# Attention and expert layers on one core: where a pair's last keys, its sums' product and its preparation stand

## The chip, the cores and the metric

The kernel runs on one core of one Trainium2 chip. The metric is the device time of one execution in microseconds (us), the median of several runs. The engines of the core are PE (TensorE, matmuls; PEld its weight loads), DVE (VectorE), ACT (ScalarE), POOL (GpSimd) and SP (SyncE, which issues all DMAs here).

## What is computed

Eight batches of attention with twelve heads, 448 tokens and head size 64, with a sigmoid in place of the softmax, and then two expert layers over all 3584 tokens (768 to 2048 to 768), with an ELU between them:

```python
scores = scale * np.matmul(q, k.transpose(0, 1, 3, 2)) - np.log(S)
attn = 1.0 / (1.0 + np.exp(-scores))
attn_out = np.matmul(attn, v)                      # (8, 12, 448, 64)
x = attn_out.transpose(0, 2, 1, 3).reshape(B * S, H * D)
h = x @ w_in
g = np.where(h > 0.0, h, np.exp(np.minimum(h, 0.0)) - 1.0)
return g @ w_out
```

## The kernel before

**Numbers.** Almost every float32 operand is scaled by a power of two and split into a high and a low float16 part, the high part by ACT and the low one by DVE (`split`, lines 135 to 137). A product is then three matmuls: high by high, low by high, high by low. Batch 0's attention alone is done in float32.

**Pairs.** A batch's twelve heads are done as six pairs of heads; the batches 1 to 7 run in the loop at the end, pair by pair (`hp` 0 to 5, called pair 0 to pair 5). The 448 keys are three tiles of 128 and a remainder of 64, the last keys. `scores(t)` (L390) multiplies key tile t by all queries on PE into a PSUM tile `psc`, of which there are two; `soften(t)` is ACT's sigmoid into `sg` (L398, four buffers); `parts(t)` splits that into `at` (ACT L434, then DVE L435). `last_keys(two)` (L477, tile `pscr`, one of the two `psc` buffers) does the remainder of two neighbouring pairs in one step, so it needs the transposed `qk` of both; its sigmoid goes into `sgr`, and `parts(NC)` splits one pair's half of it into `ar` (ACT L423, DVE L425). `values(t)` (L457) multiplies `at` and `ar` by the values into `pav`, and `finish` splits the result into `xh` on ACT and DVE (L136, L137).

**Preparation of a pair** happens two pairs ahead. DVE takes the greatest magnitudes (`mx`, L140, L318); a matmul with ones sums them over the partitions (the sums' product, tile `pr`, L128); DVE turns it into powers of two (L130, L102, L103, L328) and POOL into the scales `sc` (L334, L329, L332, L302). `scales()` is all this from the product on. `third()` then splits q and k into `nat` and v into `vn` on ACT and DVE, and issues on SP the DMA that transposes `nat` into `qk` (L362). `prepare_next()` issues on SP the loads of the pair two further on and, on DVE, the magnitudes of the next.

**Filler.** Between a pair's steps PE works on the second expert layer of the batch before: `fill(n)` issues n steps of three matmuls each (L577, `po`). An odd batch has 96 such steps (three tiles of tokens by two halves of the columns by 16), an even one 128, since the remaining 64 tokens of two batches make a tile of their own (`po_r`). A pair gets an equal share of what is left, two more in pair 0; `gap` of them stand before the late scores (11 in pair 0, else 5), the rest before the values, and `tail` of them (4, pair 5 only) behind the values.

**First expert layer.** After pair 5, `hidden` rescales the batch's `xh` on DVE (L496, L498) and `moe1` does 16 tiles f of 18 matmuls each (L547, `ph`), with ACT's exp (L559), DVE's two steps of the ELU (L561, L562), and the split into `g` one tile behind. `beside(f)` is called after tile f and holds the one preparation that is done there. Its PSUM tiles come from three buffers that `pr` and `po` share; f 3 and f 8 use others.

**Order.** Inside `tc.manual_schedule` PE, ACT, DVE and SP issue in the order in which the code is written; only POOL's order is a scheduler's. So a line that is moved moves its instructions on every queue. In batch 1, the generator `steps` still splits the second layer's weights (`step(3)` in pairs 0 and 1, the rest in pair 2), on ACT and DVE.

In a batch's even pairs the order is `scores(0)`, the last keys of two pairs, their sigmoids, `parts(0)`; in odd pairs `scores(0)`, `scores(1)` and their softening. Then come two steps of filler, `scales()`, the rest of `gap`, and the late key tiles. `works` says in which pairs a preparation is done: pairs 1 to 5, and pair 0 of batch 1.

Of the kernel before, what the change touches and what calls it, by code (L numbers as in the profile page):

```python
# [34 lines left out]
def attention_ffn(  # L35
# [13 lines left out]
    NP = H // 2  # L49
    NC = S // P  # L50
# [8 lines left out]
    EXACT = 1  # L59
# [313 lines left out]
    class Pair:  # L373
# [35 lines left out]
        def soften(self, g):  # L409
            nb = 2 if g < NC else 1  # L410
            psc = self.psc.pop(g)
            sg = sb.tile([P, 2, S], F32, tag="sg", name=f"sg{g}{self.u}", bufs=SB)
            self.sigmoid(sg[:, :nb], psc[:, :nb, :S])
            self.sg[g] = [sg]
# [53 lines left out]
    def last_keys(two):  # L468

        psc = ps.tile([P, 2, 512], F32, tag="psc", name=f"pscr{two[0].u}", bufs=2)  # L470
        o = slice(S, S + R)
        for n in range(3):
            for i, p in enumerate(two):
                hi, lo = p.qk
                kk, qq = [(hi, hi), (lo, hi), (hi, lo)][n]
                for j in range(2):
                    nc.tensor.matmul(  # L477
                        psc[rows[j ^ i], i, :S], kk[rows[j], o], qq[rows[j], :S],
                        start=(n == 0), stop=(n == 2),
                    )  # L480
        sg = sb.tile([P, 2, S], F32, tag="sg", name=f"sgr{two[0].u}", bufs=SB)
        for i, p in enumerate(two):
            p.sg[NC] = [sg, i]

        def soften():
            for i, p in enumerate(two):
                p.sigmoid(sg[:, i], psc[:, i, :S])

        return soften
# [37 lines left out]
    def moe1(b, g, xh, m, first, beside=None):  # L527
# [8 lines left out]
        for f in range(NF):  # L536
# [28 lines left out]
            if beside:  # L565
                beside(f)
# [27 lines left out]
    def out_scale(b, xs, xp, i=slice(0, NH)):  # L594
        if b % 2 == 0 and i.start == 0:
            oscs[0] = sb.tile([P, 3, NH], F32, tag="osc", name=f"osc{b}", bufs=2)
        j = b % 2
        o = oscs[0][:, j, i]
        nc.gpsimd.tensor_scalar(
            o, wop[:, i], wm[:, 0:1], 2.0 ** (XBITS - XTOP + 2 - GTOP - WTOP),  # L600
            op0=ALU.mult, op1=ALU.mult,
        )
        nc.gpsimd.tensor_scalar(o, o, xs[:, 0, NP - 1 :], xp, op0=ALU.mult, op1=ALU.mult)
        nc.gpsimd.tensor_copy(oscs[0][rows[j], 2, i], o[rows[j]])

    def moe2(b, g, wo):
        j = b % 2
        osc = oscs[0]

        def tokens(b, c):  # L610
            if c < NC:
                return out[b * S : b * S + SM].rearrange("(p c) m -> c p m", c=NC)[c]
            return out[b * S + SM : (b + 1) * S]

        def tile_of(c, i):
            if c < NC:
                return moe2_tile(
                    wo, [(slice(0, P), tokens(b, c))],
                    lambda gj, f: g[:, gj, f, c * P : (c + 1) * P],
                    osc[:, j, i : i + 1], i, f"{b}_{c}_{i}",  # L620
                )
            return moe2_tile(
                wo, [(rows[a], tokens(b - 1 + a, NC)) for a in range(2)],
                lambda gj, f: g[:, gj, f, SM:],
                osc[:, 2, i : i + 1], i, f"{b}_r_{i}",
            )

        for i in range(NH):
            for c in range(NC + j):
                yield from tile_of(c, i)  # L630
# [3 lines left out]
    def step(n):  # L634
        for _ in range(n):
            next(steps, None)
# [7 lines left out]
    def prepare_pair(n):  # L644

        if n >= len(pairs):
            return lambda: lambda: None
        b, hp = pairs[n]
        if hp == 0:
            xs_of[b] = sb.tile([P, 3, NP], F32, tag="xs", name=f"xs{b}", bufs=2)  # L650
        scales = prepare(b, hp, *loaded.pop(n), xs_of[b])

        def second():
            transposed = scales()

            def third():
                ready[n] = transposed()

            return third

        return second
# [12 lines left out]
    def pair_of(n):  # L674
        b, hp = pairs[n]
        if hp == 0:
            xh_of[b] = sb.tile([P, NK, 2, S], F16, tag="xh", name=f"xh{b}")
        return Pair(b, hp, *ready.pop(n), xh_of[b], xs_of[b])

    def hidden(b, beside=None):  # L680

        xh, xs = xh_of.pop(b), xs_of.pop(b)
        whole = rescale(b, xh, xs)
        next(whole)
        yield
        xp, xr, rest = next(whole)
        m = sb.tile([P, 2, NF], F32, tag="msc", name=f"msc{b}")

        def first():
            rest()  # L690
            moe_scales(m, xs, xr)

        moe1(b, g, xh, m, first, beside)
        yield b, xs, xp
# [13 lines left out]
    for n in range(EXACT * NP):  # L708
# [3 lines left out]
        p = pair_of(n)  # L712
# [14 lines left out]
    scales = prepare_pair(EXACT * NP + 2)  # L727
# [8 lines left out]
    def prepare_next():  # L736
        nonlocal prepared, scales
        load_pair(prepared + 2)
        prepared += 1
        scales = prepare_pair(prepared)  # L740

    def beside(f):
        nonlocal third
        if f == 3:
            third = scales()
        if f == 5:
            third()
            prepare_next()

    third = None  # L750
    E = mybir.EngineType
    with tc.manual_schedule(engines={E.PE, E.Activation, E.DVE, E.SP}):
        for b in range(EXACT, B):
            out_scale(*of_moe2, slice(0, 1 if b == EXACT else NH))
            tiles = moe2(b - 1, g, wo)
            left = NF * NH * (NC + (b - 1) % 2)

            def fill(n):
                nonlocal left
                left -= n  # L760
                for _ in range(n):
                    next(tiles, None)

            for hp in range(NP):
                share = left // (NP - hp) + (2 if hp == 0 else 0)
                tail = 4 if hp == NP - 1 else 0
                works = hp > 0 or b == EXACT
                if hp == 0:
                    two = pair_of(b * NP), pair_of(b * NP + 1)
                elif hp % 2 == 0:  # L770
                    two = pair_of(b * NP + hp), pair_of(b * NP + hp + 1)
                p = two[hp % 2]
                p.scores(0)
                if hp % 2 == 0:
                    soften = last_keys(two)
                    p.soften(0)
                    soften()
                    p.parts(0)
                    early_ones, late_ones = (0,), (1, 2)
                else:  # L780
                    p.scores(1)
                    p.soften(0)
                    p.soften(1)
                    p.parts(0)
                    p.parts(1)
                    early_ones, late_ones = (0, 1), (2,)

                gap = 11 if hp == 0 else 5
                fill(2)
                if works:  # L790
                    third = scales()
                fill(gap - 2)
                for t in late_ones:
                    p.scores(t)
                for t in late_ones:
                    p.soften(t)
                    p.parts(t)
                if hp % 2 == 0:
                    p.parts(NC)
                if works:  # L800
                    third()
                    prepare_next()
                if b == EXACT and hp < NC:

                    step(3 if hp < NC - 1 else NF)
                if hp == NP - 1:
                    h = hidden(b, beside if b + 1 < B else None)
                    next(h)
                fill(share - gap - tail)
                if hp % 2 == 0:  # L810
                    two[1].parts(NC)
                for t in range(NC + 1):
                    p.values(t)
                p.finish()
                fill(tail)
                if b == EXACT and hp == NC - 1:
                    out_scale(*of_moe2, slice(1, NH))
            of_moe2 = next(h)
        out_scale(*of_moe2)
        for _ in moe2(B - 1, g, wo):  # L820
            pass
# [30 lines left out]
```

## Time and profile before

| | us |
|---|---|
| runs | 1246.44, 1250.15, 1252.17 (median 1250.15) |
| the profiled execution | 1246.27 |
| its span, first to last instruction | 1244.5 |
| PE busy | 1162.9 (93%) |
| DVE busy | 828.8 (67%) |
| ACT busy | 722.4 (58%) |
| mean granted TensorE clock | 0.983 of full speed |

The span begins with some 174 us of start, batch 0 and the preparation of the weights. From there on a batch's six pairs and its first expert layer follow each other: pairs of batch 1 from 174, its layer from 275, pairs of batch 2 from 331, and so on to the layer of batch 7, which ends at 1177.6; the second layer of batch 7 ends the span. A row of the timeline gives start, duration, engine, line, operation, output and inputs, how many instructions, and in square brackets the idle time of the engine before it with what ended it. Durations of matmuls overlap, so that a group's length is what counts, not the mean of one. The rows that matter are shown with the prediction.

### The profile page before, as it was taken

How to read it: one execution, taken by the hardware profiler on the slowest of the kernel's cores; microseconds unless marked ns; L12 is line 12 of the kernel's file. 1: busy time of each engine (PE TensorE's matmuls, PEld its weight loads, DVE VectorE, ACT ScalarE, POOL GpSimd, SP SyncE). 2: the span in 40 equal slices, each digit the busy share in tenths (PEclk: the TensorE clock that was granted, in tenths of full speed). 3: DMA queues.
4: the chain of work that ended last, by engine and by line, in shares of the span. 5: the costliest groups of instructions: out<-in, count | busy, mean ns of one | idle time of the engine just before them, and what ended most of it. 6: DMA issues, size and time to landing. Idle time of an engine off the chain costs nothing.

```text
span 1244.5 us, 19369 instructions
## 1 busy us (share of the span) xinstructions
PE 1162.9 (93%) x7342; PEld 599.5 (48%) x7342; DVE 828.8 (67%) x1742; ACT 722.4 (58%) x1099; POOL 95.2 (8%) x275
## 2 busy tenths in 40 slices
PE   6879776899999999989999999999999999999998
PEld 2324333445555555445555554444555555445565
DVE  4897878876467765777567765777567865765500
ACT  4965777765566446764566546774466545863400
POOL 1021002010011100110011100110001000000000
PEclk9989996999999999999999999999999999999999
DMA  8945432442024410442024410343024420310000
GB/s 225 283 122 156 162 127 47 106 103 52 1 58 90 96 39 7 89 109 57 8 58 90 96 38 8 83 96 64 21 51 96 96 38 1 73 28 7 1 26 26
DMA packets 219550, 91.32 MB, mean 73 GB/s; under 512 B 183616, under 2 KB 215360, under 8 KB 219456
## 3 DMA queue, kind: packets, MB, share of 16 engines
q1 hardware_dynamic: 219456, 90.09, 30.1%
q8 instruction: 57, 0.93, 0.3%
q14 instruction: 37, 0.30, 0.1%
HBM read 59.77 MB, written 11.01 MB: 57 GB/s over the span
## 4 chain that ended last, share of the span: by engine, by line
PE 69%; DVE 12%; ACT 7%; DMA 6%; issue 2%; SPq 2%; POOL 1%; DVEq 0%; ACTq 0%
PE ph L547 31%; PE po L577 22%; PE po_r L577 5%; PE pav L457 5%; PE psc L390 5%; DMA qk<-nat 3%; ACT sg L398 2%; DVE at L435 2%; DMA stage<-in_moe_w_in_dram 2%; DVE mx L140 2%; DVE nat L137 1%; DVE ar L425 1%; PE pscr L477 1%; ACT at L434 1%; DMA wo<-in_moe_w_out_dram 1%
## 5 line engine op out<-in xcount | busy, mean ns | idle before, releaser
L547 PE MATMUL ph<-xh,wi 128*128 128x448 f16 x2304 | 445.0, 355 | 20.1 <-DVE xh L498 11.0
L577 PE MATMUL po<-wo,g 128*128 128x384 f16 x2304 | 395.5, 329 | 1.3 <-DVE al L130 1.1
L577 PEld LDWEIGHTS <-g 128*128 128x128 f16 x2688 | 254.0, 98 | 207.0 <-issue 45.7
L547 PEld LDWEIGHTS <-wi 128*128 128x128 f16 x2304 | 225.5, 98 | 237.4 <-issue 28.7
L435 DVE SCALAR_TENSOR_TENSOR at<-sg,at 128x896 f16<-128x896 f32 x126 | 135.4, 1089 | 112.4 <-ACT at L434 112.4
L559 ACT ACTIVATE e<-ph,msc 128x448 f32<-128x448 f32 x128 | 80.6, 631 | 197.0 <-PE ph L547 183.8
L398 ACT ACTIVATE sg<-psc,bias,sc 128x896 f32<-128x896 f32 x126 | 135.5, 1092 | 18.9 <-PE psc L390 16.7
L561 DVE TENSOR_SCALAR e<-e 128x448 f32<-128x448 f32 x128 | 50.2, 393 | 144.4 <-ACT e L559 144.3
L434 ACT ACTIVATE at<-sg 128x896 f16<-128x896 f32 x126 | 117.2, 948 | 2.0
L136 ACT ACTIVATE g<-e,msc 128x384 f16<-128x384 f32 (+1 forms) x192 | 96.1, 533 | 9.9 <-DVE e L562 8.7
L137 DVE SCALAR_TENSOR_TENSOR g<-e,msc,g 128x384 f16<-128x384 f32 (+1 forms) x192 | 94.8, 522 | 2.6 <-ACT g L136 2.2
L390 PE MATMUL psc<-qk 64*128 64x448 f16 x756 | 87.4, 353 | 4.1 <-ACT sg L398 4.1
L562 DVE SCALAR_TENSOR_TENSOR e<-ph,msc,e 128x448 f32<-128x448 f32 x128 | 87.4, 684 | 4.1
L136 ACT ACTIVATE nat<-raw,sc 128x384 f16<-128x384 f32 (+1 forms) x126 | 59.8, 533 | 37.6 <-POOL sc L329 27.8
L457 PE MATMUL pav<-at,vn 128*64 128x448 f16 x756 | 80.3, 358 | 0.0
L136 ACT ACTIVATE xh<-pav,sc 128x448 f16<-128x448 f32 x48 | 30.1, 628 | 77.4 <-PE pav L457 75.9
L334 POOL TENSOR_SCALAR sc<-pw 128x1 f32<-128x1 f32 x42 | 11.7, 279 | 807.1 <-DVE pw L103 761.8
L457 PEld LDWEIGHTS <-vn 128*64 128x64 f16 x924 | 49.4, 110 | 45.4 <-issue 10.1
L137 DVE SCALAR_TENSOR_TENSOR nat<-raw,sc,nat 128x384 f16<-128x384 f32 (+1 forms) x126 | 60.2, 526 | 15.1 <-ACT nat L136 14.5
L577 PE MATMUL po_r<-wo,g 128*128 128x384 f16 x384 | 64.8, 327 | 0.0
L585 DVE TENSOR_SCALAR o<-po,osc 128x384 f32<-128x384 f32 x48 | 29.4, 612 | 40.7 <-PE po L577 35.8
L390 PEld LDWEIGHTS <-qk 64*128 64x128 f16 x756 | 30.2, 94 | 52.8 <-issue 33.9
(108 smaller groups left out, 933.0 us busy)
## 6 DMA issues: line engine op xcount, KB each, us to landing
stage<-in_moe_w_in_dram SPq DMA_DIRECT2D x16, 768.0 KB, 6.3
raw<-in_q_dram SPq DMA_DIRECT2D x96, 96.0 KB, 3.3
raw<-in_k_dram SPq DMA_DIRECT2D x96, 96.0 KB, 2.9
rv<-in_v_dram SPq DMA_DIRECT2D x48, 192.0 KB, 2.8
out_dram<-o SPq DMA_DIRECT2D x48, 192.0 KB, 2.1
wo<-in_moe_w_out_dram SPq DMA_DIRECT2D x19, 384.0 KB, 4.4
so<-in_moe_w_out_dram SPq DMA_DIRECT2D x13, 384.0 KB, 4.4
rv<-in_v_dram SPq DMA_DIRECT2D x96, 32.0 KB, 2.4
```

Of the source, the lines that this page charges most:

```text
L136: nc.scalar.mul(hi, src, s)
L137: nc.vector.scalar_tensor_tensor(lo, src, s, hi, op0=ALU.mult, op1=ALU.subtract)
L390: nc.tensor.matmul(psc[:, j, :S] if g < NC else psc[rows[j], 0, :S], kk[rows[j], o], qq[rows[j], :S], start=(n == 0), stop=(n == len(parts ...
L398: a = nc.scalar.activation(to, psc, AF.Sigmoid, bias=bias, scale=self.s_scale)
L434: nc.scalar.mul(hi, sg, 2.0**ATOP)
L435: nc.vector.scalar_tensor_tensor(lo, sg, 2.0**ATOP, hi, op0=ALU.mult, op1=ALU.subtract)
L457: nc.tensor.matmul(pav[rows[j], :S], vv[i][:, 2 * NC + j if g == NC else j * NC + g], sg[k][:, j], start=(g == 0 and n == 0), stop=(g == N ...
L547: nc.tensor.matmul(ph[:, :S], wi[:, wj, c, f * P : (f + 1) * P], xh[:, c, xj], start=(n == 0), stop=(n == 3 * NK - 1),)
L559: a = nc.scalar.activation(e, ph[:, :S], AF.Exp, scale=inv)
L561: nc.vector.tensor_scalar(e, e, 1.0, -1.0, op0=ALU.min, op1=ALU.add)
L562: nc.vector.scalar_tensor_tensor(e, ph[:, :S], inv, e, op0=ALU.mult, op1=ALU.max)
L577: nc.tensor.matmul(po[:, :HM], lh(gj, f), wo[:, i, f, wj], start=(n == 0), stop=(n == 3 * NF - 1),)
```

## The change

Four edits are made in the loop over the pairs and in `beside`.

1. Every pair now begins with `scores(0)` and `scores(1)`, their softening and their parts. The last keys' scores of two pairs (in even pairs) come behind `scores(2)`, after the `gap`.
2. The sums' product (`scales()`) stands two filler steps before `scores(2)`, instead of two steps after the pair's first scores.
3. `parts(NC)` is done by each pair itself, behind `parts(2)`. Before, the even pair did both, the second one behind its filler.
4. `works` leaves out pair 5, and `beside` holds two preparations, `scales()` after f 2 and 8 and `third()` after f 4 and 10, instead of one after f 3 and 5.

```diff
     def beside(f):
         nonlocal third
-        if f == 3:
+        if f in (2, 8):
             third = scales()
-        if f == 5:
+        if f in (4, 10):
             third()
             prepare_next()
...
-                works = hp > 0 or b == EXACT
+                works = hp < NP - 1 and (hp > 0 or b == EXACT)
...
-                p.scores(0)
+                for t in range(2):
+                    p.scores(t)
+                for t in range(2):
+                    p.soften(t)
+                for t in range(2):
+                    p.parts(t)
+
+                gap = 11 if hp == 0 else 5
+                fill(gap - 2)
+                if works:
+                    third = scales()
+                fill(2)
+                p.scores(2)
                 if hp % 2 == 0:
                     soften = last_keys(two)
-                    p.soften(0)
+                p.soften(2)
+                if hp % 2 == 0:
                     soften()
-                    p.parts(0)
-                    early_ones, late_ones = (0,), (1, 2)
-                else:
-                    p.scores(1)
-                    p.soften(0)
-                    p.soften(1)
-                    p.parts(0)
-                    p.parts(1)
-                    early_ones, late_ones = (0, 1), (2,)
-
-                gap = 11 if hp == 0 else 5
-                fill(2)
-                if works:
-                    third = scales()
-                fill(gap - 2)
-                for t in late_ones:
-                    p.scores(t)
-                for t in late_ones:
-                    p.soften(t)
-                    p.parts(t)
-                if hp % 2 == 0:
-                    p.parts(NC)
+                p.parts(2)
+                p.parts(NC)
                 if works:
                     third()
                     prepare_next()
...
                 fill(share - gap - tail)
-                if hp % 2 == 0:
-                    two[1].parts(NC)
                 for t in range(NC + 1):
                     p.values(t)
```

The names in the rows below are tile, batch and pair, then a buffer number: `psc03_4` is the score tile 0 of batch 3, pair 4, `pscr3_4` that of the last keys of pairs 4 and 5.

On PE, at the start of pair 4 of batch 3, there stood before the last scores of tile 0 and then the last keys':

```order
L390 LDWEIGHTS qk3_4_5080
L390 MATMUL psc03_4_5321<-qk3_4_5080 128x448
L477 LDWEIGHTS qk3_4_5080
L477 MATMUL pscr3_4_5328<-qk3_4_5080 64x448
L477 LDWEIGHTS qk3_4_5080
L477 MATMUL pscr3_4_5328<-qk3_4_5080 64x448
L477 LDWEIGHTS qk3_5_5238
L477 MATMUL pscr3_4_5328<-qk3_5_5238 64x448
```

Now the same place goes on with the scores of tile 1, and the last keys' come behind those of tile 2:

```order
L390 LDWEIGHTS qk3_4_5080
L390 MATMUL psc23_4_5376<-qk3_4_5080 128x448
L477 LDWEIGHTS qk3_4_5080
L477 MATMUL pscr3_4_5383<-qk3_4_5080 64x448
L477 LDWEIGHTS qk3_4_5080
L477 MATMUL pscr3_4_5383<-qk3_4_5080 64x448
L477 LDWEIGHTS qk3_5_5238
L477 MATMUL pscr3_4_5383<-qk3_5_5238 64x448
```

The first instruction that reads pair 5's `qk` (`qk3_5`) has moved behind 12 matmuls of scores and 15 of filler.

On ACT, in the same pair, this was the order from the first sigmoid to the remainder's product:

```order
L398 ACTIVATE sg03_4_5342<-psc03_4_5321,bias_64,sc3_4_5026 128x896
L398 ACTIVATE sgr3_4_5341<-pscr3_4_5328,bias_64,sc3_4_5026 128x448
L398 ACTIVATE sgr3_4_5341<-pscr3_4_5328,bias_64,sc3_5_5201 128x448
L434 ACTIVATE at03_4_5346<-sg03_4_5342 128x896
L398 ACTIVATE sg13_4_5394<-psc13_4_5380,bias_64,sc3_4_5026 128x896
L434 ACTIVATE at13_4_5396<-sg13_4_5394 128x896
L398 ACTIVATE sg23_4_5399<-psc23_4_5387,bias_64,sc3_4_5026 128x896
L434 ACTIVATE at23_4_5401<-sg23_4_5399 128x896
L423 ACTIVATE ar3_4_5404<-sgr3_4_5341 64x448 x2
```

And this is the order now:

```order
L398 ACTIVATE sg03_4_5335<-psc03_4_5321,bias_64,sc3_4_5025 128x896
L398 ACTIVATE sg13_4_5337<-psc13_4_5328,bias_64,sc3_4_5025 128x896
L434 ACTIVATE at03_4_5339<-sg03_4_5335 128x896
L434 ACTIVATE at13_4_5342<-sg13_4_5337 128x896
L398 ACTIVATE sg23_4_5397<-psc23_4_5376,bias_64,sc3_4_5025 128x896
L398 ACTIVATE sgr3_4_5396<-pscr3_4_5383,bias_64,sc3_4_5025 128x448
L398 ACTIVATE sgr3_4_5396<-pscr3_4_5383,bias_64,sc3_5_5199 128x448
L434 ACTIVATE at23_4_5401<-sg23_4_5397 128x896
L423 ACTIVATE ar3_4_5404<-sgr3_4_5396 64x448 x2
```

The two sigmoids of the last keys (`sgr`) have moved from second and third place to behind the third tile's.

On DVE, at the end of pair 5 of batch 3, there stood between the third tile's part and the rescaling of `xh` (L498) a preparation of the next batch's pair 1:

```order
L435 SCALAR_TENSOR_TENSOR at23_5_5567<-sg23_5_5565,at23_5_5567 128x896
L137 SCALAR_TENSOR_TENSOR nat4_1_5570<-raw4_1_5243,sc4_1_5540,nat4_1_5570 128x384
L137 SCALAR_TENSOR_TENSOR nat4_1_5570<-raw4_1_5243,sc4_1_5540,nat4_1_5570 128x128
L137 SCALAR_TENSOR_TENSOR nat4_1_5570<-raw4_1_5243,sc4_1_5540,nat4_1_5570 128x384
L137 SCALAR_TENSOR_TENSOR vn4_1_5579<-rv1_86,sc4_1_5540,vn4_1_5579 128x512
L140 TENSOR_REDUCE mx4_2_5592<-rv0_85 128x4
L140 TENSOR_REDUCE mx4_2_5592<-raw4_2_5421 128x7
L318 TENSOR_TENSOR mx4_2_5592<-mx4_2_5592,half_81 128x2
L496 TENSOR_SCALAR rr3_5597<-xs3_3769 128x6
L498 TENSOR_SCALAR xh3_4685<-xh3_4685,rr3_5597 128x896 x5
```

Now the pair's own remainder stands there alone:

```order
L435 SCALAR_TENSOR_TENSOR at23_5_5547<-sg23_5_5545,at23_5_5547 128x896
L425 SCALAR_TENSOR_TENSOR ar3_5_5550<-sgr3_4_5396,ar3_5_5550 64x448 x2
L496 TENSOR_SCALAR rr3_5555<-xs3_3769 128x6
L498 TENSOR_SCALAR xh3_4685<-xh3_4685,rr3_5555 128x896 x5
L499 TENSOR_TENSOR xs3_3769<-xs3_3769,rr3_5555 128x5
L137 SCALAR_TENSOR_TENSOR xh3_4685<-pav3_5_5584,sc3_5_5199,xh3_4685 128x448
```

The preparation's rows (`nat4_1`, `vn4_1`, `mx4_2`) have moved into batch 3's expert layer, behind its tile f 4; those of pair 2 stand behind f 10.

## The prediction

> **What bounds the kernel now.** I read the page's first block, then the stretches by stage, then TensorE's waits, then the timeline at each wait. PE is busy for 1162.9 of 1244.5 us, so the question is where the other 81.6 us lie.
>
> ```profile
> PE 1162.9 (93%) x7342; PEld 599.5 (48%) x7342; DVE 828.8 (67%) x1742; ACT 722.4 (58%) x1099; POOL 95.2 (8%) x275
> ```
>
> By stretches of the kernel (columns as the head says, each with its count of instructions):
>
> ```profile
> core 0: us, PE busy (x) PEld busy (x) DVE busy (x) ACT busy (x) POOL busy (x), PEclk, DMA share, GB/s
> ...
> 174.00:275.40 101.40, 82.14 (x552) 40.64 (x551) 80.42 (x160) 73.83 (x111) 14.20 (x37) 0.90 0.36 83
> ...
> 331.00:421.00 90.00, 90.00 (x661) 48.52 (x657) 64.73 (x125) 62.18 (x85) 10.18 (x26) 1.00 0.36 76
> ...
> 476.20:558.70 82.50, 75.87 (x564) 39.34 (x565) 61.35 (x116) 61.51 (x83) 8.12 (x26) 1.00 0.34 75
> 558.70:614.50 55.80, 55.80 (x304) 28.61 (x307) 35.52 (x89) 24.05 (x50) 1.77 (x7) 1.00 0.18 39
> ...
> 1043.00:1123.00 80.00, 75.67 (x564) 39.40 (x563) 53.31 (x94) 57.63 (x76) 4.95 (x15) 1.00 0.17 40
> ```
>
> And PE's waits over the whole span (us in total, times, the longest):
>
> ```profile
> PE pscr L477 <- DMA qk<-nat: 14.8, 8, 2.8
> PE ph L547 <- DVE xh L498: 11.0, 4, 4.2
> ...
> PE pr L128 <- DVE mx L318: 6.0, 5, 4.5
> ```
>
> The stretches are, in order, the six pairs of batch 1, of batch 2, of batch 3, the first expert layer of batch 3, and the pairs of batch 7. Batch 2 (an even batch has four token tiles of the second layer as filler) has no idle PE at all, nor has the expert layer. The odd batches (three token tiles) leave PE idle: 6.6 us in batch 3, 4.3 in batch 7, 19.3 in batch 1. So only odd batches can gain, and the waits name two causes the change touches: the last keys' scores wait for a transposed `qk` (14.8 us, 8 times: pairs 2 and 4 of batches 1, 3, 5, 7), and the first expert layer waits for `xh` to be rescaled.
>
> The timeline of batch 3 shows the first cause, from pair 1 into pair 2:
>
> ```profile
> 490.05 1.31 PE L390 MATMUL psc<-qk 64*128 64x448 f16 x12
> ...
> 496.76 1.09 DVE L435 SCALAR_TENSOR_TENSOR at<-sg,at 128x896 f16<-128x896 f32 x1
> ...
> 497.97 1.41 ACT L136 ACTIVATE nat<-raw,sc 128x384 f16<-128x384 f32 x3 [1.24 <-POOL sc L329]
> 498.62 1.42 DVE L137 SCALAR_TENSOR_TENSOR nat<-raw,sc,nat 128x384 f16<-128x384 f32 x3 [0.77 <-ACT nat L136]
> ...
> 502.39 0.38 PE L477 MATMUL pscr<-qk 64*64 64x448 f16 x2
> 504.15 0.76 PE L477 MATMUL pscr<-qk 64*64 64x448 f16 x10 [1.38 <-DMA qk<-nat]
> ...
> 508.65 5.05 PE L577 MATMUL po<-wo,g 128*128 128x384 f16 x30
> ...
> 513.39 1.27 DVE L425 SCALAR_TENSOR_TENSOR ar<-sgr,ar 64x448 f16<-64x448 f32 x2
> 500.10 4.01 DMA qk<-nat
> ```
>
> Two of the twelve matmuls run, then PE stands until the transposition begun at 500.10 has landed: pair 3's `qk` is made in pair 1 and wanted at the first moment of pair 2.
>
> **The change, part by part.** *Last keys' scores behind the third key tile.* No instruction is added or removed. Ahead of them on PE now stand the second key tile's scores (12 matmuls of two tiles took 1.31 us, so 0.65), five filler steps of three matmuls (30 took 5.05 us, so 0.50 a step, 2.5) and the third tile's scores (0.65): 3.8 us of work that needs no new `qk`. The longest of the eight waits is 2.8. Against that, the odd pair now does its own remainder (`parts(NC)`) ahead of `nat`. On ACT it falls into idle time: ACT stood 1.24 us before `nat`. On DVE it does not: `at` ended at 497.85, the remainder takes 1.27, so `nat` starts at about 499.15 in place of 498.62, and `qk` lands 0.55 later. The worst wait asks for 2.8 + 0.55 = 3.35 of 3.8: **all 14.8 us go**, by a margin of 0.45 at the worst place. If that cover failed the cost would be what is missing, not the whole.
>
> *Sums' product later.* Its matmul `pr` waited 6.0 us for `mx` in all, 4.46 of it once in batch 1 (row below), 1.5 in the other four waits. It now comes one filler step (0.5 us) later; in even pairs the second tile's scores only take the place of the last keys' ahead of it. What hangs on it, the chain al, pw, sc on DVE, now stands behind the second `at` in every pair, as it did in the odd ones, and so after its 1.09; in the even pairs `nat` comes later still, behind the third `at` and the remainder. A gain of 0 to 1.5 us; I take 0.
>
> *A batch's last pair has no preparation.* The second cause in batch 3, at the end of pair 5:
>
> ```profile
> 552.22 1.07 DVE L435 SCALAR_TENSOR_TENSOR at<-sg,at 128x896 f16<-128x896 f32 x1
> ...
> 554.06 1.42 DVE L137 SCALAR_TENSOR_TENSOR nat<-raw,sc,nat 128x384 f16<-128x384 f32 x3 [0.77 <-ACT nat L136]
> ...
> 555.47 0.75 DVE L137 SCALAR_TENSOR_TENSOR vn<-rv,sc,vn 128x512 f16<-128x512 f32 x1
> ...
> 556.74 1.08 DVE L140 TENSOR_REDUCE mx<-raw 128x7 bf16<-128x896 f32 x1
> ...
> 558.19 1.90 DVE L498 TENSOR_SCALAR xh<-xh,rr 128x896 f16<-128x896 f16 x5
> 558.70 1.48 PE L547 MATMUL ph<-xh,wi 128*128 128x448 f16 x7 [2.25 <-DVE xh L498]
> ```
>
> Between the last `at` (ends 553.29) and the rescaling (558.19) lie 4.9 us of preparation; in its place comes 1.27 of remainder. The rescaling starts about 3.6 us earlier, more than the wait of 2.25. Of the row's 11.0 us, 4.2 belong to batch 0, which isn't touched; the 6.8 of batches 1, 3 and 5 go. What is late next: the remainder now stands in pair 5, whose values come early since four steps follow them. These rows price both sides, the page's groups first:
>
> ```profile
> L398 ACT ACTIVATE sg<-psc,bias,sc 128x896 f32<-128x896 f32 x126 | 135.5, 1092 | 18.9 <-PE psc L390 16.7
> L434 ACT ACTIVATE at<-sg 128x896 f16<-128x896 f32 x126 | 117.2, 948 | 2.0
> ...
> 504.95 1.34 ACT L398 ACTIVATE sgr<-pscr,bias,sc 128x448 f32<-128x448 f32 x2 [1.35 <-PE pscr L477]
> 513.62 1.89 PE L457 MATMUL pav<-at,vn 128*64 128x448 f16 x18
> ```
>
> PE reaches the remainder's values 1.3 (two tiles' scores) + 2.5 (five steps) + 0.65 + 3.5 (seven steps) + 1.7 (18 value matmuls, less the last one's tail) = 9.65 us into the pair. ACT starts 0.65 into it and needs 3 x 1.09 + 3 x 0.95 + 1.17 (row below), DVE 1.27 more: 9.2. I take nothing; the bound is the whole 1.27 in each of four odd batches, 5 us. It is no gain, since this work is new there.
>
> *The expert layer has two.* In six layers (batches 1 to 6) a second preparation comes at f 8 and 10, beside the one at f 2 and 4. What one does to DVE is seen in batch 3's layer:
>
> ```profile
> 581.98 1.40 DVE L137 SCALAR_TENSOR_TENSOR nat<-raw,sc,nat 128x384 f16<-128x384 f32 x3
> ...
> 585.67 0.17 DVE L318 TENSOR_TENSOR mx<-mx,half 128x2 bf16<-128x2 bf16 x1
> 585.74 0.39 DVE L561 TENSOR_SCALAR e<-e 128x448 f32<-128x448 f32 x1
> ...
> 586.37 0.63 ACT L559 ACTIVATE e<-ph,msc 128x448 f32<-128x448 f32 x1 [2.03 <-PE ph L547]
> ...
> 589.83 0.63 ACT L559 ACTIVATE e<-ph,msc 128x448 f32<-128x448 f32 x1 [2.09 <-PE ph L547]
> ```
>
> DVE is held for 3.8 us (581.98 to 585.74). A tile of the layer lasts 3.46 (586.37 to 589.83), and three PSUM tiles let PE run two tiles, 6.9 us, ahead. PE was busy for 55.80 of 55.80 us there. The second one stands six tiles, 20 us, behind the first, and DVE has 55.8 - 35.5 = 20.3 us left for it: cost nothing. Without any cover it would be 3.8 x 6 = 23 us, the other bound. Its transposition and loads on SP's queue go with it, behind the store that stood after them; the raw data of the next pair has six tiles to arrive.
>
> *Batch 1* is held by more than these two:
>
> ```profile
> 190.24 2.23 POOL L599 TENSOR_SCALAR osc<-wop,wm 128x1 f32<-128x1 f32 x2
> ...
> 201.01 0.17 PE L128 MATMUL pr<-mx,ones 128*128 128x12 bf16 x1 [4.46 <-DVE mx L318]
> ...
> 205.46 1.17 ACT L423 ACTIVATE ar<-sgr 64x448 f16<-64x448 f32 x2
> ...
> 208.18 1.30 PE L390 MATMUL psc<-qk 64*128 64x448 f16 x6 [4.10 <-ACT sg L398]
> ...
> 209.42 6.68 PE L577 MATMUL po<-wo,g 128*128 128x384 f16 x30
> ...
> 204.00:208.00 4.00, 0.08 (x1) 0.10 (x1) 3.75 (x8) 3.80 (x7) 0.00 (x0) 0.50 0.49 134
> ```
>
> There ACT and DVE still split the output weights and are full (3.80 and 3.75 of 4.00 us). The remainder of 1.17 on ACT ahead of `sg` moves into the next pair, but in pair 0 two of the weights' splits now come ahead of `nat` on ACT and DVE, and on POOL more of the output scales (`osc`) ahead of pair 2's, so `mx` is no earlier. I take nothing; bounds are 1.2 of gain at the wait of 4.10 and, the other way, the 2.23 of two `osc` at the wait of 4.46.
>
> After these waits the granted clock is 0.50, and 30 filler matmuls take 6.68 us against 5.05 in batch 3. After the 2.25 and 1.38 us waits of batch 3 the clock stayed at 1.00. The Trainium skill (TensorE: Matmul & The Clock Gate, Part 1: The HAM clock gate) says that an idle window of about 3.4 us halves the clock until a window is busy again. The trace agrees: it stays full after 2.25 and is half after 4.46. By that rule a wait cut from 4.10 to under 3.4 would give back the slow stretch too; the sum would be some 2 to 3 us lower.
>
> **Sum:** 14.8 + 6.8 = 21.6 us less. The profiled execution took 1246.27 us (span 1244.5), so the same execution of the changed kernel 1224.7. Of four known times (1246.27, 1246.44, 1250.15, 1252.17) the profiled one is the lowest, their median 1248.3 lies 2.0 above it. I forecast 1224.7 + 2.0 = 1226.7, so **1227 us**.
>
> **Rivals.** *Half is given back.* The waits move: to the remainder in pair 5 (up to 5 us), to a DVE that is late in the layer (a third of the 23, 8). Together 4 to 13 less gain, 1231 to 1240. For it: two margins of 0.45 us. Against: with batch 3's 6.6 idle us gone, DVE is still only 61.35 of 75.9 us busy, ACT 61.51, and one preparation in five is moved out of the stretch.
>
> *Batch 1 gains too.* The weights' splits let `sg` come 1.2 earlier, the idle window gets shorter, the clock returns sooner: 30 fillers at 5.05 instead of 6.68 and 1.2 + 0.8 around them: 3 to 6 more, 1221 to 1224. Against: the splits set the pace, not PE. The skill's clock gate rule is the one named above.
>
> *No change.* The second preparation finds no cover at all and costs the 23 us: 1250. The layer's 20 idle us of DVE speak against.
>
> *Slower.* In every even pair `sgr` and the remainder now start only after the third tile's scores, and the values wait for them. In pairs 2 and 4 PE needs 0.76 for the last keys, some 10 steps (5.0) and 18 value matmuls (1.7) before it wants the remainder: 7.5 us after the third tile's scores; ACT needs from there 1.09 + 1.34 + 0.95 + 1.17, DVE 1.27 more, 5.8. The margin is 1.7. To end over 0.5% (6.2 us) slower, 21 even pairs must lose 21.6 + 6.2 = 27.8, 1.3 each: the chain would have to be 3.0 us later than worked out, in even batches too, where the filler is longer. Then 1257.
>
> That the change does nothing can't be: the order of the instructions shows it.
>
> **Chances.** Forecast (1224 to 1231) 0.60, half given back 0.18, batch 1 gains too 0.10, no change 0.07, slower 0.05. The range reaches from 1219 (batch 1's gain less the scatter) to 1240. A measurement can tell about 0.5% from no change; below 1243.9 is faster: 0.88, same 0.07, slower 0.05.
>
> **What would show it.** `pscr` no longer waits for `qk` in the list of PE's waits, and `ph` for L498 only in batch 0; batches 3, 5 and 7 take some 76 us of pairs; the expert layers keep 55.8 with PE full. I am wrong if layers grow at f 10 to 14, if `pav` waits for `ar`, or if `pscr` waits for `sg` instead.

## The result, and the profile after

The changed kernel takes **1213.62 us** (median of four runs, 1213.38 to 1214.35) against 1248.89 before (four runs, 1246.44 to 1252.17): a ratio of 0.9717, 95% interval 0.9692 to 0.9742. Forecast were 1227, with a range from 1219 to 1240. The direction was right and the waits that the forecast took out are gone, but the gain is 35 us where 22 were expected, and the time lies below the range. The profiled execution took 1213.38 us, 32.9 less than the one before.

PE's waits over the whole span (us in total, times, the longest), those that answer to the rows shown before:

```profile
PE psc L390 <- ACT sg L398: 9.7, 5, 4.4
...
PE ph L547 <- DVE xh L498: 4.2, 1, 4.2
...
PE pr L128 <- DVE mx L318: 3.2, 2, 2.9
...
PE pscr L477 <- ACT sg L398: 0.2, 1, 0.2
```

`pscr` waits for `qk` nowhere, `ph` for L498 only in batch 0, and `pav` for `ar` not at all (0.9 us in batches 3, 5 and 7 before). For `sg`, which was to be a sign of being wrong, `pscr` waits once, 0.24 us in pair 2 of batch 1. By stretches (columns as in the prediction; pairs of batch 1, of batch 2, of batch 3, batch 3's expert layer, pairs of batch 7):

```profile
174.00:265.60 91.60, 78.22 (x541) 39.02 (x539) 77.65 (x153) 70.37 (x105) 15.48 (x32) 0.91 0.37 89
...
321.00:410.90 89.90, 89.90 (x660) 48.34 (x656) 60.96 (x114) 59.51 (x81) 9.54 (x21) 1.00 0.30 69
...
466.20:540.50 74.30, 74.30 (x563) 38.99 (x560) 59.10 (x109) 59.19 (x79) 9.54 (x21) 1.00 0.34 78
540.50:595.80 55.30, 55.30 (x302) 28.50 (x301) 37.19 (x96) 25.75 (x54) 2.91 (x12) 1.00 0.21 47
...
1016.00:1090.30 74.30, 74.30 (x563) 38.95 (x560) 53.07 (x94) 57.15 (x75) 7.33 (x15) 1.00 0.20 43
```

Batches 3 and 7 now run with PE busy throughout; batch 1 still leaves 13.4 us idle. Batch 3's pairs fell from 82.5 to 74.3 us, by 8.2, though only 6.6 us of idle PE stood there: PE's *busy* time fell too, from 75.87 to 74.30, with the same matmuls. So busy time had held some waiting. The layer carries its second preparation at no cost. The place where pair 1 passes into pair 2, as shown before:

```profile
490.84 1.31 PE L390 MATMUL psc<-qk 64*128 64x448 f16 x12
...
492.08 1.64 PE L577 MATMUL po<-wo,g 128*128 128x384 f16 x9
...
494.65 0.74 PE L390 MATMUL psc<-qk 64*128 64x448 f16 x6
495.32 0.76 PE L477 MATMUL pscr<-qk 64*64 64x448 f16 x12
```

The twelve matmuls of the last keys run in one piece of 0.76 us. Before, they began at 502.39 and ended at 504.91 (504.15 and 0.76): 2.52 us, so the wait cost 1.76, where its row said 1.38. The ten matmuls behind the wait take the same 0.76 us as all twelve do now, so the 0.38 us of the two ahead of it, which count as busy, were waiting too.

To see where time went I measured each pair's length in PE's timeline, from its first score matmul to that of the next pair (pair 5: to the layer's first matmul). In batches 2 to 7 these lengths repeat to some 0.05 us from one execution to the next, except where a wait for `qk` stands or the clock falls (see below). In us:

| batch 3 | pair 0 | 1 | 2 | 3 | 4 | 5 | sum |
|---|---|---|---|---|---|---|---|
| before | 14.62 | 11.67 | 14.11 | 12.71 | 15.50 | 14.66 | 83.27 |
| changed | 13.79 | 11.67 | 12.36 | 12.15 | 12.85 | 12.14 | 74.96 |
| e1_keys | 13.80 | 11.66 | 12.36 | 12.16 | 12.84 | 13.96 | 76.78 |
| e5_keys_only | 13.80 | 11.66 | 12.36 | 12.16 | 12.84 | 13.64 | 76.46 |
| e9_late_second | 14.49 | 11.67 | 12.46 | 12.51 | 13.08 | 14.43 | 78.64 |
| e6_remainder | 14.62 | 11.67 | 16.32 | 12.70 | 14.92 | 14.03 | 84.26 |
| e2_prep | 14.61 | 11.67 | 14.14 | 12.72 | 15.52 | 12.14 | 80.80 |
| e3_sums | 14.62 | 11.67 | 14.10 | 12.22 | 17.71 | 14.65 | 84.97 |
| e7_no_sums | 13.80 | 11.67 | 12.36 | 12.15 | 12.85 | 12.14 | 74.97 |

| batch 1 | pair 1 | 2 | 3 | 4 | 5 |
|---|---|---|---|---|---|
| before | 24.08 | 13.78 | 12.71 | 16.01 | 14.65 |
| changed | 21.98 | 12.71 | 12.62 | 12.84 | 12.14 |
| e1_keys | 21.79 | 13.42 | 13.11 | 12.84 | 13.97 |
| e5_keys_only | 24.27 | 12.36 | 12.48 | 12.95 | 13.67 |
| e7_no_sums | 21.97 | 13.42 | 13.11 | 12.84 | 12.14 |
| e8_gap | 19.69 | 15.25 | 12.62 | 12.85 | 12.14 |

The pairs of batches 2, 4 and 6 take 90.6 us in both kernels, but for batch 6 before, with 90.8: in its pair 4 the twelve matmuls of the last keys took 1.01 us in place of 0.76, and no wait is listed. The layers of batches 1, 3 and 5 take 54.68 in place of 54.80.

### The profile page after: what moved, and what is told of

Read it like the earlier page. It is cut to its first block, busy times and chain, and to the rows that moved or that the text cites. A ratio compares the mean times of both kernels' runs of the same rounds, so it can differ in the third digit from the quotient of the medians.

```text
span 1211.6 us, 19382 instructions
## 1 busy us (share of the span) xinstructions
PE 1156.1 (95%) x7342; PEld 598.6 (49%) x7342; DVE 826.8 (68%) x1742; ACT 719.1 (59%) x1099; POOL 107.8 (9%) x275
## 4 chain that ended last, share of the span: by engine, by line
PE 82%; DVE 6%; ACT 5%; DMA 3%; SPq 2%; issue 1%; POOL 1%; DVEq 0%; ACTq 0%; POOLq 0%
PE ph L547 32%; PE po L577 30%; PE pav L457 8%; PE psc L390 6%; PE po_r L577 5%; DMA stage<-in_moe_w_in_dram 1%; ACT sg L398 1%; PE pscr L477 1%; DMA wo<-in_moe_w_out_dram 1%; DVE wo L137 1%; SPq L268 1%; DVE wo L172 1%; ACT wo L153 1%; DVE mx L140 1%; ACT stage L157 0%
## 5 line engine op out<-in xcount | busy, mean ns | idle before, releaser
L137 DVE SCALAR_TENSOR_TENSOR xh<-pav,sc,xh 128x448 f16<-128x448 f32 x48 | 32.6, 679 | 38.9 <-ACT xh L136 38.9
```

Of the source, the lines that this page charges most:

```text
L137: nc.vector.scalar_tensor_tensor(lo, src, s, hi, op0=ALU.mult, op1=ALU.subtract)
```

## Experiments

**The four edits one by one.** First edits 1 and 3 (last keys behind the third tile, each pair its own remainder) on the kernel before, as in the change, with the product, `works` and `beside` as they were:

```diff
-                p.scores(0)
...
+                for t in range(2):
+                    p.scores(t)
...
+                p.scores(2)
+                if hp % 2 == 0:
+                    soften = last_keys(two)
+                p.soften(2)
+                if hp % 2 == 0:
+                    soften()
+                p.parts(2)
+                p.parts(NC)
```

> The kernel before with the last keys' scores behind the third key tile and each pair's own remainder (edits 1 and 3) alone. Theory 'idle rows' (a wait costs what the list of PE's waits says): the 14.8 us of pscr go, ph still waits for L498, by up to 1.27 us more in batches 1, 3, 5 since the remainder now stands in pair 5; 14.8 - 3 x 1.3 = 11 less, a profiled execution of 1235. Theory 'a wait costs more than its row' (the start of a batch's pairs to the start of its layer shrank by 8.3 us in batch 3 where the rows gave 6.6): pairs 2 and 4 of batch 3 shorten by 1.75 and 2.65 us where the rows gave 1.38 and 2.29, pair 0 by 0.8; 16 to 18 less, 1229.

1221.48 us (four runs, 1221.0 to 1222.04; ratio 0.9791, 0.9771 to 0.9812). Its profiled span of 1219.5 is 25.0 under the 1244.5 of before: more than either theory had, and 10 more than the 14.8 of the row. Pairs 2 and 4 shortened as the theory 'a wait costs more than its row' said, and pair 0 by its 0.8, but pair 3 (0.55) and pair 5 (0.7) did too, and pair 1 of batch 1 by 2.3.

Edit 4 alone:

```diff
-        if f == 3:
+        if f in (2, 8):
...
-        if f == 5:
+        if f in (4, 10):
...
-                works = hp > 0 or b == EXACT
+                works = hp < NP - 1 and (hp > 0 or b == EXACT)
```

> The kernel before with the preparations moved (edit 4) alone: pair 5 has none, the expert layer two. 'Idle rows': 6.8 less, 1239.5. 'A wait costs more': pair 5 of batches 1, 3 and 5 shorter by 2.3 to 2.6 instead of 2.25, 7.5 less, 1238.7; the layers keep 54.8 us in both. If the moved preparation itself gave more (a DVE that is ahead in later pairs), pairs 0 to 4 would shorten too: then under 1236.

1241.84 us (six runs; ratio 0.9958, 0.9944 to 0.9972). Pair 5 takes 12.14 in batches 1, 3 and 5, 2.5 less each, and no other pair is shorter by more than 0.4. That is the 7.5 of the second theory, and the layers' 0.12 each, which neither had, make it 7.9. Its profiled execution kept only 3.3 of them: in batches 1 and 5 pair 4 was 1.7 us longer than before, and pair 1 of batch 1 began 1.3 later.

Edit 2 alone:

```diff
-                fill(2)
+                fill(gap - 2)
                 if works:
                     third = scales()
-                fill(gap - 2)
+                fill(2)
```

> The kernel before with the sums' product three filler steps later in pairs 1 to 5 (nine in pair 0; edit 2) alone. 'Idle rows': at most the 1.5 us of pr's waits outside batch 1's long one, 1245 to 1246. If the product's place is what freed the extra 11 us, this one shows 5 or more less, and batch 1's pair 1 (24.1 us long before, 22.0 after) shortens by 2.

1250.41 us (ten runs, 1245.99 to 1256.57; ratio 1.0016, 0.9991 to 1.0041): no gain. Pair 3 is 0.5 shorter, and pair 4 waits that much longer for its `qk`. Pair 1 of batch 1 kept 24.1, so the product's place isn't what freed the rest.

The kernel before once more:

> The kernel before, unchanged, for a second profile. The four known times scatter from 1246.4 to 1252.2. If the scatter lies in the stretch up to batch 1's pair 2, the batches 2 to 7 and the layers keep their lengths to 0.1 us (batch 3's pairs 83.27 us); if in the waits for transposed qk, the pairs of the odd batches differ.

1245.17 us, span 1243.4. All lengths in batches 2 to 7 agree to 0.15 us with the first profile; it is 1.0 shorter up to the start of batch 1's pair 1 (193.16 and 194.16), where the changed kernel's also stands at 193.16. In the eleven profiles that point lies between 192.3 and 196.0. So 1.0 of the 32.9 us can't be told from the scatter of the start, and no scatter of batches 3 to 7 is seen in this pair of executions.

**Where the scatter is.** It shows in e3_sums, where pair 4 of batch 3 took 17.71 us, with a wait for `qk` of 2.82. In each of the eleven traces the granted clock changes only at points of a grid that are 3.413 us apart (to 0.002 us). Cut at the points of e3_sums, the stretches around its wait are these (the last three columns are the granted clock, the DMA share and GB/s):

```profile
534.91:538.32 3.41, 1.33 (x14) 0.66 (x15) 2.05 (x5) 0.63 (x2) 0.00 (x0) 1.00 0.76 152
538.32:541.73 3.41, 3.41 (x14) 1.51 (x11) 1.63 (x5) 1.65 (x3) 0.00 (x0) 0.50 0.35 74
541.73:545.15 3.42, 3.42 (x27) 1.73 (x26) 0.56 (x3) 2.42 (x3) 1.27 (x6) 1.00 0.45 135
```

PE was idle for 2.08 of the first 3.41 us, and the clock was 0.50 in the second. In e2_prep it fell in batch 5 after a wait of 2.29, the length that batch 3's had in the kernel before, where the clock stayed at 1.00. PE's timeline of e2_prep there, and its stretches:

```profile
813.07 0.76 PE L477 MATMUL pscr<-qk 64*64 64x448 f16 x10 [2.29 <-DMA qk<-nat]
813.75 1.80 PE L577 MATMUL po<-wo,g 128*128 128x384 f16 x6
...
815.42 2.64 PE L577 MATMUL po<-wo,g 128*128 128x384 f16 x9
```

```profile
810.68:814.10 3.42, 1.13 (x15) 0.48 (x14) 2.39 (x5) 1.16 (x2) 0.00 (x0) 1.00 0.86 171
814.10:817.51 3.41, 3.41 (x13) 1.67 (x12) 1.37 (x4) 1.94 (x3) 0.00 (x0) 0.50 0.50 118
```

and at the wait of batch 3 in the kernel before, with its stretches and nine fillers of pair 5:

```profile
531.87 0.76 PE L477 MATMUL pscr<-qk 64*64 64x448 f16 x10 [2.29 <-DMA qk<-nat]
...
546.37 1.62 PE L577 MATMUL po<-wo,g 128*128 128x384 f16 x9
```

```profile
526.81:530.22 3.41, 2.77 (x28) 1.15 (x24) 3.38 (x8) 2.43 (x4) 0.00 (x0) 1.00 0.38 73
530.22:533.64 3.42, 1.77 (x18) 0.95 (x19) 1.70 (x4) 1.17 (x3) 0.00 (x0) 1.00 0.66 137
533.64:537.05 3.41, 3.41 (x28) 1.64 (x27) 1.69 (x5) 2.31 (x4) 0.38 (x2) 1.00 0.56 131
```

Nine filler matmuls took 2.64 us in place of the 1.62 that nine take at full clock. The two waits are equally long and lie differently on the grid: e2_prep's falls whole into one stretch (2.29 us idle), that of the kernel before into two (0.64 and 1.65). All eleven traces agree. Of the stretches from 170 us to 1200 that ran at full clock, all 30 with over 1.91 us of idle PE were followed by one at 0.50, and none of the 3217 with under 1.81; of the seven between, three were. A fall costs 1.4 us (pair 2 of batch 3 in e6_remainder, below) to 1.7 (the two in e2_prep).

That is the scatter of the kernel before. Its times in all runs go from 1244.4 to 1256.1 us, those of the six kernels without waits for `qk` over 0.5 to 2.3 (two to four runs each). The slowest run had a mean granted clock of 0.974, one of 1244.74 us 0.983: 0.009 of 1250 us is 11 us of clock, and the times differ by 11.3.

**Which part of edits 1 and 3.** Edit 1 alone, with both remainders in the even pair:

```diff
                 p.parts(2)
-                p.parts(NC)
+                if hp % 2 == 0:
+                    p.parts(NC)
...
                 fill(share - gap - tail)
+                if hp % 2 == 0:
+                    two[1].parts(NC)
```

(the difference to e1_keys)

> As e1_keys, but both remainders stay in the even pair (edit 1 without edit 3). Theory 'place': the wait for qk alone is what edit 1 removes: pairs 2 and 4 of batch 3 at 12.4 and 12.9 us or a little more, pairs 0, 3 and 5 as before (14.6, 12.7, 14.7); some 16 of e1's 25 us. Theory 'remainder': moving the second remainder out of the even pair is what relieves DVE; then pairs 2 and 4 stay 0.5 us or more above e1's. A wait for qk still costs nothing in either.

1222.31 us (two runs; 0.9794, 0.9765 to 0.9822), span 1219.6: all of e1's gain. Neither theory had it right. Pairs 0 and 3 shorten without edit 3. What edit 3 does: pair 1 of batch 1 is 2.5 shorter with it (24.27 to 21.79), pairs 2 and 3 there 1.7 longer together, and pair 5 is 0.3 longer in the odd batches.

Edit 3 alone:

```diff
-                if hp % 2 == 0:
-                    p.parts(NC)
+                p.parts(NC)
...
-                if hp % 2 == 0:
-                    two[1].parts(NC)
```

> The kernel before with each pair's own remainder (edit 3) alone. 'Place': qk lands 0.55 us later in pairs 2 and 4, which become 14.7 and 16.0 us or more in batch 3, and, with a wait near 2.8 us, the granted clock falls to about 0.5 after some of them (2 us more each); pairs 0, 3 and 5 shorten by 0.8, 0.5 and 0.7: 0 to 5 us slower in all. 'Remainder': pairs 2 and 4 shorten as well, 5 or more faster.

1245.74 us (eight runs; 0.9972, 0.9941 to 1.0002): next to nothing. Pair 2 waits longer, as 'place' said (14.9 us in batches 5 and 7; 16.32 in batch 3, where the clock was 0.50 from 501.24 to 504.65) and pair 5 shortened, but pairs 0 and 3 kept 14.62 and 12.70, and pair 4 got shorter (14.9), which that theory had wrong. In pair 1 of batch 1 the wait for `sg` fell from 4.10 to 2.91, but the pair only from 24.07 to 23.54.

Only the last keys moved, behind the late tiles and three more filler steps, with the second tile's scores left behind the gap:

```diff
                 if hp % 2 == 0:
-                    soften = last_keys(two)
                     p.soften(0)
-                    soften()
                     p.parts(0)
...
                 if hp % 2 == 0:
+                    fill(3)
+                    gap += 3
+                    last_keys(two)()
                     p.parts(NC)
```

> The kernel before with only the last keys' scores moved: in even pairs the first tile alone stands at the start, as before, the second and third behind the gap, and the last keys' after three more filler steps; both remainders as before. Theory 'the wait alone': what shortened pairs 0, 2, 3 and 4 in the run with edit 1 alone is the removed wait for qk; then pairs 2 and 4 of batch 3 come to 12.4 to 12.9 us here too, and pair 3 to 12.2, with pair 0 at 14.6 at most. Theory 'two tiles first': the second tile's sigmoid early is what lets ACT and DVE end a pair's parts in time; then pair 0 stays at 14.6 or grows, pair 3 stays at 12.7, and the even pairs wait for their last parts: 12.9 or more in pairs 2 and 4, 1225 us or more in all against 1221.

1232.16 us (two runs; 0.9879, 0.9837 to 0.9922): both theories hold in part. Pairs 2 and 4 lose their waits (12.46, 13.08), but pair 0 stays at 14.49, pair 3 at 12.51 and pair 5 at 14.43, and batch 3 is 2.2 us longer than with edit 1 whole (e5_keys_only). ACT's waits tell why. In the list of ACT's waits, of this kernel, of before, and of the changed one:

```profile
ACT sg L398 <- PE psc L390: 22.0, 21, 1.8
```

```profile
ACT sg L398 <- PE psc L390: 17.2, 25, 1.1
```

```profile
ACT sg L398 <- PE psc L390: 0.9, 3, 0.5
```

With one tile at an even pair's start, ACT runs out of scores and stands until the gap is over. With two it works through, and the third tile's part and the remainder end earlier; what comes behind them on ACT and DVE (the preparation, `mx`, the rescaling) is earlier too. In pair 0 of batch 3 that shows directly. Before, the values' end waited for the remainder:

```profile
487.03 1.89 PE L457 MATMUL pav<-at,vn 128*64 128x448 f16 x18
488.93 0.35 PE L457 MATMUL pav<-ar,vn 128*64 128x448 f16 x1
489.58 0.54 PE L457 MATMUL pav<-ar,vn 128*64 128x448 f16 x3 [0.30 <-DVE ar L425]
490.05 1.31 PE L390 MATMUL psc<-qk 64*128 64x448 f16 x12
```

After, it doesn't:

```profile
476.97 1.89 PE L457 MATMUL pav<-at,vn 128*64 128x448 f16 x18
478.69 0.55 PE L457 MATMUL pav<-ar,vn 128*64 128x448 f16 x4
479.17 1.31 PE L390 MATMUL psc<-qk 64*128 64x448 f16 x12
```

From the first value matmul to the next pair it took 3.02 us and takes 2.20: 0.82 less. Of that 0.18 stands ahead of the first remainder matmul (1.90 us behind the first value matmul before, 1.72 after) and isn't listed; the wait listed with 0.30 cost the other 0.64. DVE starts the remainder (L425) 12.8 us into this pair before, 12.7 in e9_late_second and 11.9 in e5_keys_only. The three more filler steps aren't what keeps it late in e9: there ACT, once the second tile's scores have come, goes without a wait through to the remainder:

```profile
478.88 1.10 ACT L398 ACTIVATE sg<-psc,bias,sc 128x896 f32<-128x896 f32 x1 [0.95 <-PE psc L390]
...
484.06 2.23 ACT L423 ACTIVATE ar<-sgr 64x448 f16<-64x448 f32 x4
484.65 1.27 DVE L425 SCALAR_TENSOR_TENSOR ar<-sgr,ar 64x448 f16<-64x448 f32 x2 [0.60 <-ACT ar L423]
```

**Do the parts add up?** The changed kernel without edit 2:

```diff
-                fill(gap - 2)
+                fill(2)
                 if works:
                     third = scales()
-                fill(2)
+                fill(gap - 2)
```

> The changed kernel with the sums' product where it was, two steps behind the first scores (edits 1, 3 and 4 without 2). If the parts add up (25.0 for edits 1 and 3, 7.9 for edit 4, 0 for edit 2, by the stretches), 1213 to 1214 us, and pair 3 of batch 3 up to 0.5 longer at most. If edit 2 is needed beside the others, 2 or more slower than the changed kernel.

1215.61 us (two runs; 0.974, 0.9712 to 0.9768), span 1213.6 against 1211.6. Batches 2 to 7 are the same to 0.05 us. In batch 1, pairs 2 and 3 take 26.53 in place of 25.33: 1.2 us that edit 2 is worth there, beside the others, where alone it was worth nothing; the other 0.8 lie ahead of pair 1, where executions scatter.

**A version beyond both?** The changed kernel with filler in place of the waits in batch 1's pair 1:

```diff
                 gap = 11 if hp == 0 else 5
+                if b == EXACT and hp == 1:
+                    gap = 13
```

> The changed kernel with 13 filler steps in place of 5 ahead of the third key tile in pair 1 of batch 1, where PE waits 2.92 us for the sums' magnitudes and 4.43 for a score tile. If PE's filler can fill these waits, pair 1 (21.98 us) shortens by 2 to 3 us and the kernel takes 1211. If the splits of the weights on ACT and DVE set its end anyway, it stays within 0.5 us of the changed kernel, 1213.5.

1213.57 us (two runs; 0.9724, 0.9695 to 0.9752), the changed kernel's time. Pair 1 is 2.3 shorter and pair 2 is 2.5 longer: its product and its third tile now wait.

```profile
216.90 0.17 PE L128 MATMUL pr<-mx,ones 128*128 128x12 bf16 x1 [0.83 <-DVE mx L318]
...
219.58 0.74 PE L390 MATMUL psc<-qk 64*128 64x448 f16 x6 [1.52 <-ACT sg L398]
```

PE's filler fills the wait, and ACT and DVE, which are behind with the weights, make PE wait later.

## Why the prediction was right in direction and wrong in size

*The wait for `qk` goes:* right, at all eight places. The cover is the 3.8 us that were worked out: in pair 2 of batch 3 the last keys' scores begin 4.48 us into the pair in place of 0.67. At the tightest place, pair 4 of batch 1, the transposition is issued at 240.13 and takes some 4.0 us (median of the 42 in this trace), so it lands 0.8 ahead of the matmuls at 244.95, where 0.45 were forecast. The size was wrong. The term "14.8" was read from the idle column. By the pairs' lengths, pairs 2 and 4 gave 4.2 in batch 1 and 4.4 in each of batches 3, 5 and 7: **17.4**. A row's idle time begins where the last matmul's modelled end lies, not where the next would have started, and so each wait counted 0.3 to 0.4 too little.

*The wait for the rescaling goes:* right. The term "6.8" measured **7.5** (2.5 three times), for the same reason. The remainder that now stands in pair 5 costs nothing that stays (pair 5 of batch 7, which had no preparation before either, takes 12.14 us in both kernels); with the preparation there it would (e5 to e1, 0.3 us).

*The second tile's scores "only take the place of the last keys'", and "I take 0":* this is the step that failed in its mechanism. The prediction used the second tile's scores only as cover, put the gain at the product's waits for `mx` at 0, and had no term for pair 0's wait for `ar`. That two tiles at the start keep ACT supplied was not seen, though 16.7 of the 18.9 us of ACT's idle time before `sg` are put to `psc` in the very row that was quoted for a duration. It took away pair 0's wait for `ar` (2.5 us in batches 3, 5, 7) and pair 3's for `mx` (1.8 in all). e9_late_second shows the first: there pair 0 keeps 14.49 of its 14.62 us. The second is less plain: of pair 3's 0.56 us a batch 0.2 comes in e9 too, without the second tile, and edit 2 alone takes 0.49 away (e3_sums).

*Batch 1, "I take nothing", bounds 1.2 and 2.23:* 2.1 us came in pair 1, outside the bound. They hang on edit 3, the remainder that no longer stands ahead of pair 1's `sg` on ACT (24.27 in e5, 21.79 in e1). Edit 3 alone brings the 1.2 at the wait for `sg` that the bound had, and 0.5 of the pair's length (e6_remainder). There the pair's listed waits are 7.37 us in all, as in the changed kernel (7.36), but 13.65 us of it run at half clock, in place of 10.24, and it is 1.6 us longer; before, 13.65 us ran at half clock too. That points to the clock for most of the rest, but doesn't show it: e1_keys has 6.83 us at half clock and is hardly shorter (21.79 and 21.98).

*The expert layer takes the second preparation:* right. The layers even lose 0.12 us.

*The scatter, "+ 2.0":* wrong. The median of the kernel before lay above its profiled execution because the clock was lower in the runs that took longer; the traces of e2_prep and e3_sums show it falling at waits for `qk` and for the rescaling. In the profiled execution it fell nowhere between pair 1 of batch 1 and the last microsecond. With the waits the scatter went: the changed kernel's median is 0.24 above its profiled execution. The offset belonged to waits that the prediction itself removed.

*The clock gate:* the Trainium skill's rule (TensorE: Matmul & The Clock Gate, Part 1: The HAM clock gate) of an idle window of about 3.4 us was read as a limit on the length of a wait: full after 2.25 us, half after 4.46. The traces don't bear that reading out: a wait of 2.29 us halved the clock in e2_prep and left it full in the kernel before. What counted was the idle time inside one stretch of the grid, and 1.8 to 1.9 of its 3.41 us were enough. The trace that the prediction was read from has such a place too: the clock fell at 185.47, behind a stretch with 1.85 us idle.

The sum of the profiled executions: 17.4 + 7.5 + 2.5 (pair 0) + 1.8 (pair 3) + 2.1 (batch 1, pair 1) + 1.0 (the start's scatter) + 0.7 (layers 0.4, batch 6's pair 4 0.3) = 33.0, against 32.9 measured and 21.6 forecast. By edits: 1 and 3 gave 25.0 (e1_keys); on top of them edit 4 gave 5.9 more (pair 5 three times 1.83, the layers 0.4), since e1 had already taken 0.7 of the 2.5 of each pair 5; edit 2 gave the 1.0 by which pairs 1 to 3 of batch 1 shortened from e1 to the changed kernel; and the 1.0 of the start lies in no edit. Of the rivals, 'batch 1 gains too' came in part (2.1 us of its 3 to 6); the others did not: no wait took the place of those removed.

## What to carry to other kernels

Read what a wait costs as the distance between the matmuls around it, less what the same stretch takes where nothing waits, not from the idle column. When an edit moves work forward, ask what it supplies as well as what it covers: an engine off the critical path that stands waiting for a moved product will run ahead and take later waits away. Where runs scatter, compare their mean granted clocks and look for waits behind which the clock falls, before adding the scatter to a forecast.

## What the runs showed of the hardware

The granted clock changed only on a grid of 3.413 us (eleven traces). A stretch of the grid at full clock with over 1.91 us of idle PE was followed by one at 0.50 in 30 of 30 cases, one with under 1.81 in none of 3217. So equal waits of 2.29 us halved the clock where they lay in one stretch (e2_prep, batch 5) and not where they were split into 0.64 and 1.65 (the kernel before, batch 3), and each fall cost 1.4 to 1.7 us. A wait of PE cost 0.3 to 0.4 us more than the idle time listed for it (2.52 - 0.76 = 1.76 us at a wait listed with 1.38; 0.64 at one of 0.30).
